# Attention and MLP kernel, second sweep: the second MLP layer in Strassen's form from the third group on, four first-layer products in one PSUM bank, and a written order for four engines

## The chip, the cores and the metric

The kernel is one program on one core of a Trainium2 chip. Its time is the device time of one launch in microseconds (us). The engines that matter here are TensorE (PE in the profile, with its weight loads as PEld), VectorE (DVE), ScalarE (ACT), GpSimd (POOL) and SyncE (SP), whose queue issues the transfers. SBUF is the on-chip memory that all engines read, PSUM the banks into which TensorE accumulates; a bank here holds 128 partitions of 512 fp32 values.

## The reference

The kernel computes an attention layer with a decay (8 batches, 8 heads, 576 tokens, 64 dimensions per head), a low-rank mixing over the tokens, and then an MLP. Only the MLP is touched:

```python
xt = x.transpose(0, 2, 1)
h = xt @ U @ V                       # mixing over tokens
u = x + h.transpose(0, 2, 1)
ch = np.maximum(u @ w_ch1, 0.0) @ w_ch2
return (u + ch).astype(np.float32)   # 8 x 576 x 512
```

`w_ch1` is 512 x 2048 and `w_ch2` 2048 x 512. All is fp32. Every matrix product is made from two rounded parts of each operand, a high part and a low part (`h` and `l`, type fp32r): high times high, low times high and high times low, so three matmuls stand for one.

## The kernel before

There are two sweeps. The first does attention and mixing and, of the MLP, the first 6 of the 16 chunks of 128 hidden units; it leaves `u` in two parts (`ud`) and the sum so far (`accd`) in DRAM. The second sweep does the other 10 chunks. It begins about 753 us into the profiled execution, works on 9 groups of 512 tokens in the order 7, 0, 1, ..., 5, 8, 6, and is written from line 945 on.

The first group is computed plainly, chunk by chunk (`first`, line 979, then `second`, line 993). From the second group on, two chunks at a time form a 2 x 2 block problem: the weights of a pair of chunks are cut into two halves of the input dimension and two chunks, the tokens into two halves of 256. Strassen's scheme in Winograd's form then makes the first layer with seven block products instead of eight. A block product is `product`: 6 matmuls that move 256 columns each (line 1069). The sums of weight blocks that it needs are made once (`weight_sums`), those of tokens once for each group: `token_sums` (lines 1052 to 1057) adds the two parts of `u` and combines the four quarters on POOL, and `token_part` splits a sum into two parts (`split`, lines 182 and 185: a copy on ACT, a subtraction on POOL). The products M1, M6, M5, M2, M7, M4, M3 of `pair_of_chunks` go into six PSUM banks in turn; line 1100 copies M1 on ACT, the seven `plus` (line 1092) combine them on DVE, and `relu` (lines 970 and 971) turns the four quarters into hidden values: the high part by ACT, the low part by DVE.

The second layer is plain in every group. `second` multiplies 128 tokens of hidden values by the 512 columns of `w_ch2`, three matmuls for each chunk (line 993). The calls of one pair of chunks wait in the list `ready` and are issued between the products of the next pair: three calls after M5, three after M7, two after M3. That makes 42 matmuls of 256 columns and 24 of 512 columns for a pair, and five pairs for a group. Four PSUM banks hold the sums of a group; when a group is complete, line 997 adds `accd` on DVE and lines 999 to 1002 store the result.

TensorE's order is the order of the text (`manual_schedule(engines={ET.PE})`); a planner orders the other engines. Each engine works through its own queue in order. Line 962 loads both parts of `u` for the next group into one of two buffers, and line 1138 loads `accd`.

Of the kernel before, what the change touches and what calls it, by code (L numbers as in the profile page):

```python
# [18 lines left out]
DM = H * D  # L19
DFF = 4 * DM  # L20
RK = 32
P = 128
# [18 lines left out]
def tile_decay_attention_moe(ctx, tc, qk, v, f, U, V, w1, w2, out):  # L41
# [908 lines left out]


    pool = pools(left, "left")
    up = pool("up", 2)
    hp_ = pool("hp", 4)
    psO = ctx.enter_context(tc.tile_pool(name="psO", bufs=4, space=PSUM, reuse_waits="tile"))
    psX = ctx.enter_context(tc.tile_pool(name="psX", bufs=2, space=PSUM, reuse_waits="tile"))
    HT = MAIN // 2

    def load_u(g):
        t = up.tile([P, 2, NDC, MAIN], F32R, tag="u", name=f"u{g}")  # L960
        for x in range(2):
            nc.sync.dma_start(t.bitcast(F32)[:, x], ud[g, :, x])
        return t[:, 0], t[:, 1]

    def hidden(name):
        return hp_.tile([P, MAIN], F32R, tag="hh", name=f"bh{name}"), hp_.tile([P, MAIN], F32R, tag="hl", name=f"bl{name}")

    def relu(h, src, cols):
        hh, hl = h[0][:, cols], h[1][:, cols]
        nc.scalar.activation(hh, src, AF.Relu)  # L970
        nc.vector.scalar_tensor_tensor(hl, src, 0.0, hh.bitcast(F32), op0=ALU.max, op1=ALU.subtract)  # L971

    def first(g, u, i):

        ps = psF.tile([P, 512], F32, tag="F", name=f"Hb{g}_{i}")
        m = 0
        for c in range(NDC):
            for wt_, ut in ((b1h, u[0]), (b1l, u[0]), (b1h, u[1])):
                nc.tensor.matmul(ps, wt_[i][:, c], ut[:, c, 0:MAIN], start=m == 0, stop=m == 3 * NDC - 1)  # L979
                m += 1  # L980
        h = hidden(f"{g}_{i}")
        relu(h, ps, slice(0, MAIN))
        return h

    def second(z, i, h, x):

        k = z["done"][x]
        z["done"][x] += 1
        if k == 0:
            z["po"][x] = psO.tile([P, DM], F32, tag="O", name=f"O{z['g']}_{x}")  # L990
        po = z["po"][x]
        for m, (ht, wt_) in enumerate(((h[0], b2h), (h[1], b2h), (h[0], b2l))):
            nc.tensor.matmul(po, ht[:, P * x : P * x + P], wt_[i], start=k == 0 and m == 0, stop=k == NB - 1 and m == 2)  # L993
        if k < NB - 1:
            return
        g, o = z["g"], z["acc"][:, x]
        nc.vector.tensor_tensor(o, po, o, op=ALU.add)
        if g < B:
            nc.sync.dma_start(out[g, P * x : P * x + P], o)
        else:  # L1000
            nc.sync.dma_start(out[2 * x + 1, MAIN:S], o[0:64])
            nc.sync.dma_start(out[2 * x, MAIN:S], o[64:128])


    n3 = 3 * 2 * P
    homes = [(sf.tile([P, 3, n3], F32R, tag=tag, name=f"sw{tag}")) for tag in ("hh", "hl")]
    more = [stp.tile([P, 1024], F32R, tag="raw", name=f"sw{x}") for x in range(3)]
    SW = []
    for i in range(NB // 2):
# [9 lines left out]
    Th = sf.tile([P, 4, 2, HT], F32R, tag="uh", name="Th")  # L1019
    Tl = sf.tile([P, 4, 2, HT], F32R, tag="ul", name="Tl")  # L1020
    tmp = [sf2.tile([P, 2, HT], F32, tag="ost", name=f"sum{x}") for x in range(2)]
    tmp.append(sf.tile([P, 2, HT], F32, tag="TS", name="sum2"))
    tmp = [t[:, y] for t in tmp for y in range(2)]

    def block(i, r, c):
        return [w[2 * i + r][:, 2 * c : 2 * c + 2] for w in (b1h, b1l)]

    def weight_sums(i, tmp=tmp):
        def whole(dst, r, c):
# [15 lines left out]
    whole_u = xn[2][:, 0:4].rearrange("p q (c t) -> p q c t", c=2)  # L1045

    def token_sums(u):

        for q in range(4):
            c, t = 2 * (q // 2), HT * (q % 2)  # L1050
            h, l = (x[:, c : c + 2, t : t + HT].bitcast(F32) for x in u)
            nc.gpsimd.tensor_tensor(whole_u[:, q], h, l, op=ALU.add)  # L1052
        b11, b12, b21, b22 = (whole_u[:, q] for q in range(4))
        nc.gpsimd.tensor_tensor(b11, b12, b11, op=ALU.subtract)
        nc.gpsimd.tensor_tensor(b12, b22, b12, op=ALU.subtract)
        nc.gpsimd.tensor_tensor(b22, b22, b11, op=ALU.subtract)
        nc.gpsimd.tensor_tensor(b21, b21, b22, op=ALU.subtract)

    def token_part(q):
        split(Th[:, q], Tl[:, q], whole_u[:, q], nc.scalar, nc.gpsimd)  # L1060

    T1, T3, T4, T2 = ([x[:, q] for x in (Th, Tl)] for q in range(4))

    def product(bank, tag, name, a, b):
        ps = bank.tile([P, 512], F32, tag=tag, name=name)[:, 0:HT]
        m = 0
        for c in range(2):
            for x, y in ((0, 0), (1, 0), (0, 1)):
                nc.tensor.matmul(ps, a[x][:, c], b[y][:, c], start=m == 0, stop=m == 5)  # L1069
                m += 1  # L1070
        return ps

    def pair_of_chunks(z, u, i, ready, renew):

        def go(k):
            for fn in ready[:k]:
                fn()
            del ready[:k]  # L1080

        def ub(c, t):
            return [x[:, 2 * c : 2 * c + 2, HT * t : HT * t + HT] for x in u]

        def f(k, a, b):
            return product(psF, "F", f"M{k}_{g}_{i}", a, b)

        def x(k, a, b):
            return product(psX, "X", f"M{k}_{g}_{i}", a, b)

        def plus(dst, ps, other):
            nc.vector.tensor_tensor(dst, ps, other, op=ALU.add)  # L1092

        g = z["g"]
        S1, (S2, S3, S4) = block(i, 1, 0), SW[i]
        h = [hidden(f"{g}_{2 * i + r}") for r in range(2)]
        lo, hi = slice(0, HT), slice(HT, MAIN)
        s1, s2, s3, s4, c11, c2 = tmp
        m1 = f(1, block(i, 0, 0), ub(0, 0))
        nc.scalar.copy(s1, m1)  # L1100
        m6 = x(6, S2, T2)
        if renew:
            token_part(3)
        plus(s2, m6, s1)
        m5 = f(5, S1, T1)
        if renew:
            token_part(0)
        plus(s4, m5, s2)
        go(3)
        plus(c11, x(2, block(i, 0, 1), ub(1, 0)), s1)  # L1110
        m7 = f(7, S3, T3)
        if renew:
            token_part(1)
        plus(s3, m7, s2)
        plus(c2, m5, s3)
        relu(h[0], c11, lo)
        relu(h[1], c2, hi)
        go(3)
        plus(s3, x(4, block(i, 1, 1), T4), s3)
        if renew:  # L1120
            token_part(2)
        plus(s4, x(3, S4, ub(1, 1)), s4)
        relu(h[1], s3, lo)
        relu(h[0], s4, hi)
        go(len(ready))
        for r, y in ((0, 0), (0, 1), (1, 2), (1, 3), (1, 0), (1, 1), (0, 2), (0, 3)):
            ready.append(lambda r=r, y=y: second(z, 2 * i + r, h[r], y))


    order = [B - 1, *range(B - 2), B, B - 2]  # L1130
    u = cur
    ready = []
    with tc.manual_schedule(engines={ET.PE}):
        for n, g in enumerate(order):
            un = load_u(order[n + 1]) if n + 1 < NG else None
            acc = xn[(n + 1) % 2]
            if n:
                nc.sync.dma_start(acc[:, 0:NM], accd[g].rearrange("x p d -> p x d"))
            z = {"g": g, "acc": acc, "po": [None] * NM, "done": [0] * NM}
            if n == 0:  # L1140
                for i in range(NB):
                    h = first(g, u, i)
                    for fn in ready:
                        fn()
                    ready = [lambda z=z, x=x, i=i, h=h: second(z, i, h, x) for x in range(NM)]
                    if i % 2 and i < 6:
                        weight_sums(i // 2)
                    if i == NB - 3:
                        token_sums(un)
                for q in (3, 0, 1, 2):  # L1150
                    token_part(q)
            else:
                for i in range(NB // 2):
                    pair_of_chunks(z, u, i, ready, un and i == NB // 2 - 1)
                    if n == 1 and i < 2:
                        spare = xn[2].rearrange("p c d -> p (c d)")
                        weight_sums(3 + i, [spare[:, 256 * y : 256 * y + 256] for y in range(5)])
                    if i == 2 and un:
                        token_sums(un)
            u = un  # L1160
        for fn in ready:
            fn()
    left.close()
    right.close()

# [45 lines left out]
```

## Time and profile before

| | |
|---|---|
| median of 3 runs | 1244.18 us (1242.86 to 1244.63) |
| profiled execution | 1242.59 us, of which the span of the profile is 1240.8 us |
| granted TensorE clock in it | 0.999 |
| TensorE busy | 1204.0 us, 97% of the span |
| VectorE, ScalarE, GpSimd busy | 861.3, 645.5 and 424.5 us |

The profile lists, for groups of instructions, the source line, the engine, the tiles written and read, the count, the busy time and the mean duration, and what ended the idle time before them. Recorded durations of matmuls overlap, so the rate of TensorE is read from the starts of its matmuls and not from their durations.

### The profile page before, as it was taken

Reading aid. Unit: us, or ns where it says so; the run is one execution under the profiler, and the core shown is the slowest. Engines: PE = TensorE matmul, PEld = TensorE weight load, DVE = VectorE, ACT = ScalarE, POOL = GpSimd, SP = SyncE. Lnnn points to the kernel's source line nnn. Section 1 sums busy time; section 2 is a strip of 40 time slices with the busy share of each in tenths; the row PEclk is TensorE's granted clock in tenths of the full one; section 3 lists DMA queues with packets and bytes.
Section 4 is the critical chain, followed back from the end, with each engine's and each line's share of the span. In section 5 each row is a group of like instructions: output and inputs, shape, how many; then the busy total and the mean of one; then the engine's idle time right before and its main releaser. Section 6 shows DMA issues by size and latency. Waiting matters only on the chain.

```text
span 1240.8 us, 21851 instructions
## 1 busy us (share of the span) xinstructions
PE 1204.0 (97%) x7824; PEld 1066.0 (86%) x7824; DVE 861.3 (69%) x2195; ACT 645.5 (52%) x1741; POOL 424.5 (34%) x377
## 2 busy tenths in 40 slices
PE   8998999999999999999999999989999999999998
PEld 5776898998989988989989888878988889888897
DVE  8877778768778778787686799684554645546443
ACT  5777678767778758777675444322122221212211
POOL 4223454534544435454541000441341413315100
PEclk9999999999999999999999999999999999999999
DMA  6544344525335325425342345121120312213010
GB/s 183 153 132 130 79 105 111 151 68 159 95 89 164 88 78 148 117 71 171 79 125 76 120 141 229 34 69 69 68 102 35 136 43 95 85 52 137 1 35 35
DMA packets 67581, 125.87 MB, mean 101 GB/s; under 512 B 7408, under 2 KB 31984, under 8 KB 65424
## 3 DMA queue, kind: packets, MB, share of 16 engines
q1 hardware_dynamic: 67408, 124.47, 32.8%
q8 instruction: 62, 1.02, 0.3%
q14 instruction: 47, 0.39, 0.1%
q10 hardware_dynamic: 64, 0.00, 0.0%
HBM read 88.65 MB, written 35.78 MB: 100 GB/s over the span
## 4 chain that ended last, share of the span: by engine, by line
PE 82%; DVE 8%; ACT 6%; issue 2%; DMA 2%; SPq 0%; ACTq 0%; POOL 0%; DVEq 0%; POOLq 0%
PE O L993 20%; PE M L1069 16%; PE A L700 10%; PE B L718 9%; PE V L543 5%; PE T L440 3%; PE S L344 3%; PE Hb L979 2%; PE V L515 2%; PE S L345 2%; ACT P L373 1%; ACT G L309 1%; PE Tt L609 1%; PE St L344 1%; PE S L341 1%
## 5 line engine op out<-in xcount | busy, mean ns | idle before, releaser
L1092 DVE TENSOR_TENSOR sum<-M,sum 128x256 f32<-128x256 f32 x280 | 117.7, 422 | 173.3 <-PE M L1069 172.3
L970 ACT ACTIVATE bh<-sum 128x256 fp32r<-128x256 f32 x160 | 66.3, 418 | 256.9 <-DVE sum L1092 256.8
L373 ACT ACTIVATE P<-S,nm 128x128 f32<-128x128 f32 (+3 forms) x256 | 137.5, 539 | 57.5 <-DVE nm L365 48.3
L365 DVE CUSTOM_DVE_ANT_0 S<-S,mask 128x128 f32<-128x128 f32 (+3 forms) x256 | 125.7, 495 | 53.5 <-PE S L345 46.8
L993 PE MATMUL O<-b2h,bh 128*128 128x512 f32 x360 | 143.0, 397 | 0.0
L993 PE MATMUL O<-b2l,bh 128*128 128x512 f32 x360 | 142.4, 396 | 0.0
L993 PE MATMUL O<-b2h,bl 128*128 128x512 f32 x360 | 141.8, 394 | 0.0
L700 PE MATMUL A<-uh,w1h 128*128 128x256 f32 (+1 forms) x384 | 120.3, 313 | 1.8 <-DVE hl L704 1.7
L309 POOL CAST G<-qk 64x576 fp32r<-64x576 f32 x52 | 34.9, 671 | 250.1 <-PE St L345 149.5
L700 PE MATMUL A<-ul,w1h 128*128 128x256 f32 (+1 forms) x384 | 113.5, 296 | 0.0
L700 PE MATMUL A<-uh,w1l 128*128 128x256 f32 (+1 forms) x384 | 113.5, 296 | 0.0
L185 POOL TENSOR_TENSOR Tl<-xn,Th 128x512 fp32r<-128x512 f32 x32 | 41.3, 1303 | 201.7 <-PE M L1069 178.1
L971 DVE SCALAR_TENSOR_TENSOR bl<-sum,bh 128x256 fp32r<-128x256 f32 x160 | 92.4, 581 | 19.4 <-ACT bh L970 19.0
L1052 POOL TENSOR_TENSOR xn<-u 128x512 f32<-128x512 f32 x32 | 43.7, 1391 | 167.6 <-DVE b1l L71 106.4
L718 PE MATMUL B<-w2h,hh 128*128 128x512 f32 x216 | 90.4, 418 | 2.3 <-DVE hl L704 1.3
L440 PE MATMUL T<-ident,P 128*128 128x128 f32 x544 | 85.5, 273 | 0.0
L718 PE MATMUL B<-w2l,hh 128*128 128x512 f32 x216 | 85.1, 394 | 0.0
L718 PE MATMUL B<-w2h,hl 128*128 128x512 f32 x216 | 84.6, 392 | 0.0
L422 DVE TENSOR_TENSOR PTl<-T,PTh 128x512 fp32r<-128x512 f32 (+1 forms) x156 | 79.0, 524 | 6.6 <-ACT PTh L419 6.3
L993 PEld LDWEIGHTS O<-b2l,bh 128*128 128x128 f32 x360 | 67.7, 188 | 16.5
L322 POOL TENSOR_TENSOR G<-qk,G 64x576 fp32r<-64x576 f32 x52 | 74.4, 1431 | 15.6 <-ACT G L309 6.2
L993 PEld LDWEIGHTS O<-b2h,bl 128*128 128x128 f32 x360 | 68.2, 189 | 11.2
(240 smaller groups left out, 3543.7 us busy)
## 6 DMA issues: line engine op xcount, KB each, us to landing
qk<-in_qk_dram SPq DMA_DIRECT2D x104, 288.0 KB
u<-ud SPq DMA_DIRECT2D x16, 1024.0 KB
sr<-in_w_dram SPq DMA_DIRECT2D x20, 512.0 KB
vr<-in_v_dram SPq DMA_DIRECT2D x32, 256.0 KB
accd<-ost SPq DMA_DIRECT2D x32, 256.0 KB
xn<-accd SPq DMA_DIRECT2D x8, 1024.0 KB
out_dram<-xn SPq DMA_DIRECT2D x32, 256.0 KB
ud<-uh SPq DMA_DIRECT2D x7, 1024.0 KB
```

Source lines behind the costliest of these rows:

```text
L322: pin(el.tensor_tensor(g[oth, 2, cols], k[oth], gf[oth, 2, cols], op=ALU.subtract))
L365: nc.vector.tensor_tensor_reduce(ps[:, :w], ps[:, :w], mask[:, 512 - w : 512], scale=-SCALE, scalar=3.0e38, op0=ALU.add, op1=ALU.min, accu ...
L373: nc.scalar.activation(pt, ps[:, :w], AF.Exp, bias=z["nm"][:, col : col + 1], scale=-1.0, accum_out=z["sm"][:, col : col + 1])
L422: defer(2, lambda: nc.vector.tensor_tensor(dstl, src, dsth.bitcast(F32), op=ALU.subtract))
L440: nc.tensor.transpose(tp[:, P * x : P * x + P], z["P"][j][i][:, P * c : P * c + P], ident)
L700: nc.tensor.matmul(ps[:, :nt], wt[:, fc, c], ut[:, c, sl], start=m == 0, stop=m == 3 * NDC - 1)
L718: nc.tensor.matmul(ps, ht[:, fc, P * x : P * x + P], wt[:, fc], start=fc == 0 and m == 0, stop=fc == NA - 1 and m == 2,)
L970: nc.scalar.activation(hh, src, AF.Relu)
L971: nc.vector.scalar_tensor_tensor(hl, src, 0.0, hh.bitcast(F32), op0=ALU.max, op1=ALU.subtract)
L993: nc.tensor.matmul(po, ht[:, P * x : P * x + P], wt_[i], start=k == 0 and m == 0, stop=k == NB - 1 and m == 2)
L1069: nc.tensor.matmul(ps, a[x][:, c], b[y][:, c], start=m == 0, stop=m == 5)
L1092: nc.vector.tensor_tensor(dst, ps, other, op=ALU.add)
```

## The change

It concerns the second sweep alone.

- From the third group on, the second layer is made in Strassen's form too (`output_products`). The hidden values X11, X12, X22 and four sums S1, S2, S3, S4 of the quarters (X21 itself is not multiplied) are multiplied with weight blocks in seven products N1 to N7 of 6 matmuls with 256 columns. Over the five pairs of a group, N1, N3, N4, N5, N6 and N7 accumulate in six banks; N2 goes into a bank of the first layer and is added to the result by DVE in every pair. At the end of a group the banks are combined into the four quarters of the result (`ends_1`, `ends_6`, `ends_3` and two single additions) by ACT, DVE and POOL.
- The second group keeps the plain second layer (`plain_products`); meanwhile `weight_sums2` makes the sums of the second layer's weights on POOL, DVE and ACT.
- In the first layer M1, M6, M7 and M4 accumulate one after another in a bank A, which ACT copies out (`s1`, `u2`, `u3`, `r12`) after each; M2, M5 and M3 share a bank B. The seven additions of a pair become three.
- The sums S3, S1, S2, S4 are made from tiles of the pair before, after M1, N1, M2 and N4 of the next pair: DVE makes the sum, ACT the high part, POOL the low part.
- The order in a pair is M1, N1, M2, N4, M6, N2, N7, M7, N5, M5, N6, M4, N3, M3. From the third group on DVE, ACT and POOL, too, keep the order of the text.
- The tokens are no longer loaded whole into a double buffer: three quarters are loaded into a tile `direct`, refilled in the last pair of a group, and the high and low part of all four go into two of the `xn` tiles, where POOL adds them (`token_whole` after the third pair's M4, `token_sums` after the fourth's).

```diff
+    def relu(h, l, src):
+        nc.scalar.activation(h, src, AF.Relu)
+        nc.vector.scalar_tensor_tensor(l, src, 0.0, h.bitcast(F32), op0=ALU.max, op1=ALU.subtract)
...
+    def weight_sums2(i):
+        eng = nc.gpsimd
...
+        for src, (h, l) in zip((t1, t0, t2, t3), [block2(i, 0, 1)] + SD[i]):
+            split(h, l, src, nc.scalar, eng)
...
+    def add(dst, a, b, eng=nc.vector):
+        eng.tensor_tensor(dst, a, b, op=ALU.add)
...
+    def output_products(z, i):
...
+        def one(k, a, w):
+            if k == 2:
+                ps = z["B"].rearrange("p (y d) -> p y d", y=2)
+                multiply(ps, a, w, True, True)
+                add(quarter[0], ps, quarter[0])
+                return
...
+        def ends_1():
+            nc.scalar.copy(u4, z["M"][1])
+            add(quarter[0], u4, quarter[0], nc.gpsimd)
+
+        def ends_6():
+            add(u4, z["M"][6], u4)
+            add(u3, z["M"][7], u4)
+            add(u4, z["M"][5], u4)
+            for q in (2, 3):
+                add(quarter[q], u3, quarter[q], nc.gpsimd)
+            for x in (2, 3):
+                store(z["g"], acc, x)
+
+        def ends_3():
+            add(quarter[1], z["M"][3], quarter[1])
+            add(quarter[1], u4, quarter[1], nc.gpsimd)
...
+        product(A, block(i, 0, 0), D1, True)
+        nc.scalar.copy(s1, A)
+        sum_(0)
+        if renew:
+            load_direct(renew, 0)
+        second_layer()
+        sum_(1)
+        ends()
+        product(Bk, block(i, 0, 1), D2, True)
+        add(c11, Bk, s1)
+        nc.scalar.activation(X11[0], c11, AF.Relu)
+        sum_(2)
...
+        second_layer()
+        nc.vector.scalar_tensor_tensor(X11[1], c11, 0.0, X11[0].bitcast(F32), op0=ALU.max, op1=ALU.subtract)
+        sum_(3)
+        ends()
+        product(A, W2, T2, False)
+        nc.scalar.copy(u2, A)
...
+        second_layer()
+        ends()
+        second_layer()
+        ends()
+        product(A, W3, T3, False)
+        nc.scalar.copy(u3, A)
...
+        product(Bk, W1, T1, True)
+        add(c22, Bk, u3)
+        nc.scalar.activation(X22[0], c22, AF.Relu)
...
+        product(A, block(i, 1, 1), T4, False)
+        nc.scalar.activation(r12, A, AF.Relu)
+        nc.scalar.copy(X12[0], r12)
...
+        second_layer()
+        nc.vector.tensor_tensor(X12[1], r12, X12[0].bitcast(F32), op=ALU.subtract)
+        ends()
+        product(Bk, W4, D3, False)
+        add(r21, Bk, u2)
...
+        nc.scalar.activation(r21, r21, AF.Relu)
+
+        def sum_0():
+            nc.vector.scalar_tensor_tensor(c22, c22, 0.0, r21, op0=ALU.max, op1=ALU.add)
+            nc.vector.scalar_tensor_tensor(r21, c11, 0.0, r21, op0=ALU.max, op1=ALU.subtract)
+            split(*S3, r21, nc.scalar, nc.gpsimd)
+
+        def sum_2():
+            nc.vector.scalar_tensor_tensor(n2, c11, 0.0, c22, op0=ALU.max, op1=ALU.subtract)
+            split(*S2, n2, nc.scalar, nc.gpsimd)
+
+        def sum_3():
+            add(r12, r12, n2)
+            split(*S4, r12, nc.scalar, nc.gpsimd)
+
+        held["sums"] = [sum_0, lambda: split(*S1, c22, nc.scalar, nc.gpsimd), sum_2, sum_3, None]
...
+        for n in range(1, NG):
+            with tc.manual_schedule(engines={ET.PE} if n == 1 else {ET.PE, ET.DVE, ET.Activation, ET.Pool}):
+                group(n)
```

More of the change, by code (lines that the diff above doesn't have):

```diff
@@ L980, in first, with store @@
                 m += 1
-        h = hidden(f"{g}_{i}")
-        relu(h, ps, slice(0, MAIN))
-        return h
[L985 to L997, printed above, removed]
+        flat = hb.rearrange("p k x t -> p (k x t)")[:, 2 * MAIN * (i % 3) : 2 * MAIN * (i % 3) + 2 * MAIN]
+        h = flat[:, 0:MAIN], flat[:, MAIN : 2 * MAIN]
+        relu(*h, ps)
+        return h
+    def store(g, acc, x):
+        o = acc[:, x]
         if g < B:
@@ L1002, in second @@
             nc.sync.dma_start(out[2 * x, MAIN:S], o[64:128])
+    def second(z, i, h, x):
+        if i == 0:
+            z["po"][x] = psM.tile([P, DM], F32, tag=BANKS[x], name=f"O{z['g']}_{x}")
+        po = z["po"][x]
+        for m, (ht, wt_) in enumerate(((h[0], b2h), (h[1], b2h), (h[0], b2l))):
+            nc.tensor.matmul(po, ht[:, P * x : P * x + P], wt_[i], start=i == 0 and m == 0, stop=i == NB - 1 and m == 2)
+        if i < NB - 1:
+            return
+        o = z["acc"][:, x]
+        nc.vector.tensor_tensor(o, po, o, op=ALU.add)
+        store(z["g"], z["acc"], x)
     n3 = 3 * 2 * P
@@ L1068, in product @@
             for x, y in ((0, 0), (1, 0), (0, 1)):
-                nc.tensor.matmul(ps, a[x][:, c], b[y][:, c], start=m == 0, stop=m == 5)
+                nc.tensor.matmul(
+                    ps, a[x][:, c], b[y][:, c], start=start and m == 0, stop=m == 5, skip_group_check=not start
+                )
                 m += 1
[L1071 to L1078, printed above, removed]
-                fn()
[L1080 to L1101, printed above, removed]
+    def add(dst, a, b, eng=nc.vector):
+        eng.tensor_tensor(dst, a, b, op=ALU.add)
@@ new lines, in plain_products, with one @@
+    def plain_products(z, i):
+        acc = z["acc"]
+        def one(x, r, h):
+            if i == 0 and r == x // 2:
+                z["M"][x] = psM.tile([P, DM], F32, tag=BANKS[x], name=f"O{z['g']}_{x}")
+            ps = z["M"][x]
+            for m, (p_, wt_) in enumerate(((0, b2h), (1, b2h), (0, b2l))):
+                nc.tensor.matmul(
+                    ps, h[p_][:, P * (x % 2) : P * (x % 2) + P], wt_[2 * i + r],
+                    start=i == 0 and r == x // 2 and m == 0, stop=i == NK - 1 and r != x // 2 and m == 2,
+                )
+            if i == NK - 1 and r != x // 2:
+                add(acc[:, x], ps, acc[:, x])
+                store(z["g"], acc, x)
+        work = [(x, r, h) for r, h, xs in ((0, X11, (0, 1)), (1, X22, (2, 3)), (1, X12, (0, 1)), (0, S3, (2, 3))) for x in xs]
+        return [(lambda y=y: one(*y), None) for y in work]
@@ new lines, in tile_decay_attention_moe, with pair_of_chunks, second_layer, ends @@
+    held = {}
+    pairs = [0]
+    def pair_of_chunks(z, i, ready, renew, plain, late):
+        g = z["g"]
+        W1, (W2, W3, W4) = block(i, 1, 0), SW[i]
+        D1, D2, D3 = ([direct[:, k, x] for x in range(2)] for k in range(3))
+        s1, u2, u3, c11, c22, r21, n2, r12 = tmp
+        pairs[0] += 1
+        if pairs[0] % 2:
+            c11 = other
+        bank_a = psX.tile([P, 512], F32, tag="A", name=f"A{g}_{i}")
+        bank_b = psX.tile([P, 512], F32, tag="B", name=f"B{g}_{i}")
+        if ready and len(ready) == 7:
+            held["z"]["B"] = bank_b
+        A, Bk = bank_a[:, 0:HT], bank_b[:, 0:HT]
+        places = 7 if len(ready) > 4 else 1
+        todo = []
+        def second_layer():
+            nonlocal places
+            n = -(-len(ready) // max(places, 1))
+            places -= 1
+            todo.extend(ready[:n])
+            del ready[:n]
+            for fn, _ in todo:
+                fn()
+        def ends():
+            for _, fn in todo:
+                if fn:
+                    fn()
+            del todo[:]
+        sums = held.pop("sums", [None] * 5)
+        def sum_(k):
+            if sums[k]:
+                sums[k]()
+        product(A, block(i, 0, 0), D1, True)
[10 more added lines that the diff above has]
+        sum_(2)
+        if renew:
+            load_direct(renew, 1)
+        second_layer()
[4 more added lines that the diff above has]
+        nc.scalar.copy(u2, A)
+        sum_(4)
@@ L1109, in pair_of_chunks @@
[L1109 to L1119, printed above, removed]
+        second_layer()
+        nc.vector.scalar_tensor_tensor(X22[1], c22, 0.0, X22[0].bitcast(F32), op0=ALU.max, op1=ALU.subtract)
+        ends()
+        product(A, block(i, 1, 1), T4, False)
@@ L1130, in tile_decay_attention_moe @@
+        def sum_2():
[5 more added lines that the diff above has]
+        held["sums"] = [sum_0, lambda: split(*S1, c22, nc.scalar, nc.gpsimd), sum_2, sum_3, None]
+        held["z"] = z
+        ready.extend(output_products(z, i))
     order = [B - 1, *range(B - 2), B, B - 2]
-    u = cur
     ready = []
-    with tc.manual_schedule(engines={ET.PE}):
[L1134 to L1161, printed above, removed]
-            fn()
```

171 lines of the change are left out of this document (134 added, 37 removed).

## The prediction, made blind

> **What bounds the kernel now.** I read the page first, then the second sweep by windows, the chain of waits in order of time, and TensorE's instructions one by one.
>
> ```profile
> span 1240.8 us, 21851 instructions
> PE 1204.0 (97%) x7824; PEld 1066.0 (86%) x7824; DVE 861.3 (69%) x2195; ACT 645.5 (52%) x1741; POOL 424.5 (34%) x377
> ```
> ```profile
> core 0: us, PE busy (x) PEld busy (x) DVE busy (x) ACT busy (x) POOL busy (x), PEclk, DMA share, GB/s
> 805.00:857.00 52.00, 48.56 (x299) 43.56 (x298) 36.13 (x77) 14.08 (x35) 17.57 (x14) 0.97 0.12 41
> 910.00:963.00 53.00, 53.00 (x332) 47.62 (x331) 27.45 (x61) 12.68 (x30) 15.89 (x12) 1.00 0.21 80
> ```
> ```profile
> 861.76 2.13 PE M L1069 x18
> ...
> 872.32 2.13 PE M L1069 x18
> ...
> 882.88 2.13 PE M L1069 x18
> ...
> 1230.15 7.02 PE O L993 x30
> ```
>
> In a group TensorE is busy for 53.00 of 53.00 us, while DVE (27.45), ACT (12.68) and POOL (15.89) have room. The chain holds nothing but matmuls and repeats every 10.56 us (861.76, 872.32, 882.88): that is a pair of chunks, and 52.8 us a group. Only the second group's start (805 to 857) shows TensorE idle, 3.4 us. So a matmul taken away in the third and later groups is gained in full, as long as no other engine then holds TensorE up.
>
> **The matmuls saved.** TensorE's rows, by their starts:
>
> ```profile
> 1225.04 0.28 PE L1069 MATMUL M<-u,b1h 128*128 128x256 f32 x1
> ...
> 1226.46 0.40 PE L993 MATMUL O<-b2h,bh 128*128 128x512 f32 x1
> ...
> 1228.56 0.28 PE L1069 MATMUL M<-Th,b1h 128*128 128x256 f32 x1
> ```
>
> Twelve matmuls of 256 columns took 1226.46 - 1225.04 = 1.42 us, 0.118 each; nine of 512 took 2.10, 0.233 each. A pair is 42 x 0.118 + 24 x 0.233 = 10.57, as the chain says. Now it is 84 x 0.118 = 9.94 (a product of six takes 0.71), 0.63 less. Strassen pairs: four from the third group (its first still issues plain products), thirty from the last six groups, and one behind the last group: 35 x 0.63 = 22 us less. This term is firm: the new matmuls have the form of those at line 1069, with a weight load for each.
>
> **What must now be ready in time.** Before, the products took six banks in turn and none waited for the reader of the one just before. Now bank A must be copied out by ACT (`u2`) between M6 and M7, and that copy stands in ACT's queue behind the high parts of S3, S1, X11, S2 and S4. Each of these follows a DVE operation, and four POOL subtractions of 128x256 run between them. The durations:
>
> ```profile
> L970 ACT ACTIVATE bh<-sum x137: 412/418/420, 860.9 to 1220.1; 128x256 fp32r<-128x256 f32 x137
> L1100 ACT COPY sum<-M x35: 372/372/376, 862.6 to 1221.8; 128x256 f32<-128x256 f32 x35
> ```
> ```profile
> L1092 DVE TENSOR_TENSOR sum<-M,sum x240: 404/424/426, 863.3 to 1223.2; 128x256 f32<-128x256 f32 x120
> ```
> ```profile
> L971 DVE SCALAR_TENSOR_TENSOR bl<-sum,bh x138: 411/424/1486, 860.7 to 1220.5; 128x256 fp32r<-128x256 f32 x138
> ```
> ```profile
> L185 POOL TENSOR_TENSOR Tl<-xn,Th x32: 1288/1296/1482, 804.0 to 1177.3; 128x512 fp32r<-128x512 f32 x32
> L185 POOL TENSOR_TENSOR VS<-vr,VS x26: 1548/1568/1574, 137.5 to 671.5; 128x640 fp32r<-128x640 f32 x26
> ```
> ```profile
> 872.16 0.28 PE L1069 MATMUL M<-u,b1h 128*128 128x256 f32 x1
> ...
> 873.12 0.38 ACT L1100 COPY sum<-M 128x256 f32<-128x256 f32 x1 [0.78 <-PE M L1069]
> ...
> 876.39 0.28 PE L1069 MATMUL M<-u,b1h 128*128 128x256 f32 x1
> ...
> 877.30 0.42 DVE L1092 TENSOR_TENSOR sum<-M,sum 128x256 f32<-128x256 f32 x1 [1.08 <-PE M L1069]
> ...
> 877.35 1.30 POOL L1056 TENSOR_TENSOR xn<-xn 128x512 f32<-128x512 f32 x1
> ...
> 877.75 0.42 ACT L970 ACTIVATE bh<-sum 128x256 fp32r<-128x256 f32 x1 [4.26 <-DVE sum L1092]
> ...
> 878.02 0.42 DVE L1092 TENSOR_TENSOR sum<-M,sum 128x256 f32<-128x256 f32 x1 [0.30 <-PE M L1069]
> ...
> 878.36 0.57 DVE L971 SCALAR_TENSOR_TENSOR bl<-sum,bh 128x256 fp32r<-128x256 f32 x1
> ...
> 878.73 1.36 POOL L1057 TENSOR_TENSOR xn<-xn 128x512 f32<-128x512 f32 x1
> ```
>
> The row of `bl` matters most: 0.42 us, but up to 1.49, while the DVE row that reads PSUM (L1092) never passes 0.426. Operations with both inputs in SBUF are the ones that stretch, when POOL is at work: at 878.36 one starts inside a POOL instruction that ends at 878.65, and ends 0.28 later, at 878.93; the next POOL instruction then lasts 1.36 instead of 1.30 and starts 0.08 behind, so POOL loses about 0.15. Five of the new DVE operations ahead of `u2` have both inputs in SBUF (c22, r21, n2, X11's low part, r12+n2).
>
> [...]
>
> From the rows above: from the end of a product's slot to its reader 0.20 on DVE (876.39 + 0.71, 877.30), 0.25 on ACT; between engines 0.04 (877.72 to 877.75); DVE starts its next operation 0.34 after the last (878.02, 878.36), and I take ACT alike. No POOL operation of 128x256 is in the trace: half of the 1.296 gives 0.65, the straight line through 512 and 640 columns 0.75. Starting at M1 of a steady pair, with 0.65 (0.75 behind the stroke):
>
> ```
> DVE r21 .20-.62   ACT relu .66-1.08   DVE c22 1.12, r21 1.46-1.88   ACT S3 1.92-2.34
> POOL S3 low 2.38-3.03 / 3.13          ACT S1 2.25-2.67
> DVE c11 (M2 ends 2.13) 2.33-2.75      ACT X11 2.79-3.21
> DVE n2 from 2.79, held by S3 low, to 3.31 / 3.41        ACT S2 to 3.77 / 3.87
> POOL S1 low 3.18-3.83 / 3.28-4.03     DVE X11 low from 3.25, held, to 4.11 / 4.31
> POOL S2 low 3.98-4.63 / 4.18-4.93     DVE r12+n2 from 4.05, held, to 4.91 / 5.21
> ACT S4 4.95-5.37 / 5.25-5.67          ACT u2 to 5.66 / 5.96
> ```
>
> M7 is due after seven products, at 4.98, and gets bank A at 5.70 or 6.00: it waits 0.72 or 1.02 in every pair. Without POOL in the way the same chain ends with `u2` at 4.76, and M7 waits for nothing. So the bounds are 0 and 1.02; I take 0.65, nearest to the lower figure, since the chain credits no slack at any hop. For 34 pairs that is 22 us (0 to 35): **the matmul saving is spent there.** What is queued behind the late `u2` is `u3`, X22 and so on, which wait for later products anyway, and TensorE's own queue.
>
> **The change of groups**, six times. POOL's addition of `ends_1` (1.30) stands between the low parts of S1 and S2, so r12+n2 ends 0.65 later: 0.6 more at M7. At the end of the pair DVE has, from N6's end as zero, the three additions of `ends_6` (128x512, 0.68 each, the second reading the first's result) to 2.2, then X12's low part, held by POOL's addition (1.7 to 3.0) to 3.28, `ends_3` to 3.88 and r21 to 4.22. M2 of the next pair needs bank B, which r21 reads, at 5 x 0.71 = 3.56 and starts at 4.28: 0.7. The relu ends at 4.68, and the next sum meets POOL's last addition (4.45 to 5.75) and ends at 6.03 instead of 5.14, on the way to S3 and again to `u2`: 1.2. Together 2.5, six times 15 us; without POOL's hold DVE's queue alone gives r21 at 3.48, in time, so the bounds are 0 and 20. The 0.68 and the end of the kernel:
>
> ```profile
> 1235.09 2.79 DVE L997 TENSOR_TENSOR xn<-O,xn 128x512 f32<-128x512 f32 x4 [3.57 <-PE O L993]
> ```
> ```profile
> 1236.75 0.40 PE L993 MATMUL O<-b2l,bh 128*128 128x512 f32 x1
> ```
>
> **The end.** Now DVE ends at 1237.88, 0.9 after the last matmul's slot (1236.75 + 0.23), and the stores follow. Then the last seven products have nothing between them: N7 must wait for S3's low part (3.03 against 2.13), about 1 us. After N6 come 1.6 us of DVE and three POOL additions, 3.9 us, before the last store: 0.2 + 1.6 + 3.9 - 0.7 (N3 runs meanwhile) = 5.0, 4 more than now. I take 6 with some queueing (4 to 8).
>
> **Once only.** `weight_sums2` of the last pair runs in the third group: eight POOL operations of 0.65 ahead of S3's low part, 1.5 us (0 to 3). The start of the second group:
>
> ```profile
> 818.41 0.38 PE L1069 MATMUL M<-Th,swhh 128*128 128x256 f32 x1 [2.59 <-DVE sum L1092]
> ```
> ```profile
> 806.58 2.93 DVE L1031 TENSOR_TENSOR xn<-b1h,b1l 128x256 f32<-128x256 f32 x2 [0.41 <-POOL Tl L185]
> ```
>
> TensorE waits 2.59 us behind DVE sums that POOL held (two took 2.93). The text keeps that meeting; fewer DVE additions there, but tokens that come through a tile which is in use until about 795. I take 0, bounds -4 and +3.
>
> **Transfers at nothing.**
>
> ```profile
> 860.43 0.79 SPq L962 DMA_DIRECT2D u<-ud  x2
> ```
> ```profile
> 869.05 5.42 POOL L1052 TENSOR_TENSOR xn<-u 128x512 f32<-128x512 f32 x4 [7.42 <-DMA u<-ud]
> ```
>
> Two MB were there 8.6 us after their issue. Each quarter of `direct` is 0.5 MB, is issued as soon as its product has run in the last pair, and is due a pair later, 9.9 us; the whole loads have more than a pair. SP's queue holds the stores ahead of them, all early in the group. Without that cover a late quarter would cost what it is late, up to some 2 us a group.
>
> **Sum.** -22 + 22 + 15 + 6 + 1.5 + 0 = +22.5 on the profiled execution's own 1242.6, so 1265.1; the median of the runs stands 1.6 above that execution, hence **1267 us**.
>
> **Rivals.**
>
> *The waits are hidden* (faster). If the three DVE operations meet no POOL instruction, M7 waits for nothing and the group change costs little: -22 + 0 + 2 + 6 + 0.5 = -13.5, so 1231. For it: the chain without POOL ends 0.2 us in time, and two second-layer products stand between M6 and M7. Against: POOL's operations start from the same ACT results, so they fall into the same microseconds; and in the row above `bl` was caught by POOL up to its full length. It decides at `u2`: ending before 4.9 us of a pair, or after.
>
> *Only the group changes pay* (the same). POOL's operations turn out shorter than 0.6 and the steady pair runs at 9.94, but 128x512 additions stay at 1.30: -22 + 0 + 15 + 6 + 1 = 0, so 1244 to 1247. For it: group changes have measured lengths, the 128x256 one is a guess.
>
> *The saving isn't there* because matmuls of 256 columns cost more than half of 512: 0.118 against 0.117 excludes it.
>
> **How the numbers follow.** A change under 0.2% (2.5 us) can't be told from none here. Forecast (1254 to 1285 by its bounds, most of it below 1280): 0.57. Waits hidden (1226 to 1240): 0.30. Group changes alone (1240 to 1250): 0.13, of which 0.05 within 0.2%, 0.04 above and 0.04 below. Slower 0.61, the same 0.05, faster 0.34. The range takes 1230 to 1280: it leaves out the lower third of the second case (0.10) and the top of the first (0.07).
>
> **What would show it.** In the changed profile: 256-column products for the second layer at 0.118 each (the 22); `bl`-like DVE rows with both inputs in SBUF at a mean near 0.7 with POOL busy; TensorE idle before M7, released by ACT's copy of A, about 0.65 in nearly every pair, and a steady period of 10.6; idle before M2 in a group's second pair, released by DVE. A period of 9.9 to 10.0 with no such idle time would prove the forecast wrong at its main step; idle time released by a DMA would be a mistake about the transfers.

## The result and the profile after

The changed kernel takes **1298.79 us** (median of four runs, 1297.38 to 1300.58) against 1244.41 for the kernel before on the same chip: a ratio of 1.044, with a 95% interval of 1.0422 to 1.0458. That is slower, as forecast, but by 54 us where 23 were forecast, and above the range (1230 to 1280). The profiled execution took 1299.44 us, with a span of 1297.7 against 1240.8, so 56.9 us more.

The page of the kernel after, and one window of its second sweep (busy time and count of PE, PEld, DVE, ACT and POOL, granted clock of TensorE, share of the DMA engines, GB/s):

```profile
span 1297.7 us, 23855 instructions
PE 1213.6 (94%) x8454; PEld 1098.1 (85%) x8454; DVE 929.9 (72%) x2209; ACT 739.8 (57%) x2028; POOL 612.6 (47%) x585
```
```profile
910.00:963.00 53.00, 47.39 (x372) 45.93 (x371) 31.47 (x52) 21.30 (x57) 32.41 (x32) 0.97 0.27 90
```

In the window that TensorE filled before (53.00 of 53.00) it is now idle for 5.6 us, and GpSimd has gone from 15.9 to 32.4 busy. Where TensorE waits is in the view of waits (the line that waits, the instruction that ends the wait, us in total, times, longest):

```profile
PE A L1103 <- ACT sum L1249: 34.8, 35, 1.8
PE B L1103 <- DVE xn L1109: 5.7, 7, 1.1
...
PE Hb L985 <- DVE xn L728: 1.2, 1, 1.2
```

The first row is the wait that the prediction named: M7 (line 1103, bank A) behind ACT's copy `u2` (line 1249). One of the 35, 0.46 us, is in the second group; the other 34 are in the 34 pairs that the prediction counted, 1.01 us each and not 0.65. The second is M2 behind r21: once in the second group (0.45), and at each of the six changes of groups (5.2 us together).

The span divides by the starts of M1, the first of the kernel before, the second of the kernel after:

```profile
806.06 0.28 PE L1069 MATMUL M<-u,b1h 128*128 128x256 f32 x1
...
861.60 0.28 PE L1069 MATMUL M<-u,b1h 128*128 128x256 f32 x1
...
914.42 0.28 PE L1069 MATMUL M<-u,b1h 128*128 128x256 f32 x1
...
1178.56 0.28 PE L1069 MATMUL M<-u,b1h 128*128 128x256 f32 x1
...
1220.81 0.28 PE L1069 MATMUL M<-u,b1h 128*128 128x256 f32 x1
```
```profile
809.86 0.28 PE L1103 MATMUL A<-direct,b1h 128*128 128x256 f32 x1
...
868.11 0.28 PE L1103 MATMUL A<-direct,b1h 128*128 128x256 f32 x1
...
925.54 0.28 PE L1103 MATMUL A<-direct,b1h 128*128 128x256 f32 x1
939.06 0.28 PE L1103 MATMUL A<-direct,b1h 128*128 128x256 f32 x1
952.24 0.28 PE L1103 MATMUL A<-direct,b1h 128*128 128x256 f32 x1
963.45 0.28 PE L1103 MATMUL A<-direct,b1h 128*128 128x256 f32 x1
974.38 0.28 PE L1103 MATMUL A<-direct,b1h 128*128 128x256 f32 x1
985.51 0.28 PE L1103 MATMUL A<-direct,b1h 128*128 128x256 f32 x1
...
1221.55 0.28 PE L1103 MATMUL A<-direct,b1h 128*128 128x256 f32 x1
1269.93 0.28 PE L1103 MATMUL A<-direct,b1h 128*128 128x256 f32 x1
```

| stretch | before | after | more |
|---|---|---|---|
| up to the second group | 806.06 | 809.86 | 3.8 |
| second group | 55.5 | 58.2 | 2.7 |
| third group | 52.8 | 57.4 | 4.6 |
| groups four to eight | 264.1 | 296.0 | 31.9 |
| ninth group, four pairs | 42.2 | 48.4 | 6.1 |
| last pair and end | 20.0 | 27.8 | 7.8 |

A group is 52.8 us before and 59.2 after. Its rows above show two kinds of pairs: the first two take 13.52 and 13.18, the other three 11.21, 10.93 and 11.13, where 10.56 was the old pair and 9.94 would be the new one without a wait.

**One steady pair**, the one that starts at 952.24, in the timeline of the kernel after. Lines 185, 1297, 1245 and 1109 are the low parts of S3, S1 and S2 (a row with x3), n2, X11's low part and r12+n2; 182 is the high part of S4:

```profile
954.80 2.49 POOL L185 TENSOR_TENSOR hb<-xn,hb 128x256 fp32r<-128x256 f32 x3 [7.13 <-ACT hb L182]
...
955.00 0.82 DVE L1297 SCALAR_TENSOR_TENSOR xn<-xn,xn 128x256 f32<-128x256 f32 x1
955.75 0.95 DVE L1245 SCALAR_TENSOR_TENSOR hb<-other,hb 128x256 fp32r<-128x256 f32 x1
956.63 0.95 DVE L1109 TENSOR_TENSOR xn<-xn 128x256 f32<-128x256 f32 x1
...
957.61 0.41 ACT L182 CAST hb<-xn 128x256 fp32r<-128x256 f32 x1 [1.35 <-DVE xn L1109]
957.92 0.37 ACT L1249 COPY sum<-A 128x256 f32<-128x256 f32 x1
...
958.35 0.39 PE L1103 MATMUL A<-Th,swhh 128*128 128x256 f32 x1 [0.93 <-ACT sum L1249]
```

This pair follows the chain of the prediction, instruction by instruction: three DVE operations, each started inside a GpSimd subtraction and each ended after it (0.82, 0.95, 0.95 where 0.42 is the undisturbed length), then S4's high part, then `u2`, then M7. From M1 the prediction had bank A free at 5.70 or 6.00; `u2` ends at 6.05 (957.92 + 0.37 - 952.24). M7 was due at 5.0 and starts at 6.11: 1.1 late. Its own product takes 0.82 instead of 0.71, since the first matmul behind the wait is 0.1 longer (the next starts 0.22 after it, at 958.57, instead of 0.12). Together 1.2, and 10.0 + 1.2 is the pair of 11.21.

The third pairs of groups four to nine and the last two pairs of the ninth group, where no token sums run, are all like this one: three held operations, M7 starting 6.1 after M1, and 11.2 for each of those that a next pair follows. The fourth and fifth pairs of the other groups (10.93 and 11.13) reach nearly the same wait by another way. There n2 and X11's low part run nearly undisturbed (0.42 and 0.45 to 0.50), and of the three only r12+n2 is held (0.95). But r21 starts 0.82 and 1.08 after M1 instead of 0.20, because the token sums on GpSimd, operations of 128x512, hold X12's low part of the pair before, here ahead of the fifth pair, which starts at 974.38:

```profile
974.07 1.46 DVE L1279 TENSOR_TENSOR hb<-xn,hb 128x256 fp32r<-128x256 f32 x1
```

### The profile page after: what moved, and what is told of

The parts are those of the page before. It is cut to its first block, busy times and chain, and to the rows that moved or that the text cites. A ratio compares the mean times of both kernels' runs of the same rounds, so it can differ in the third digit from the quotient of the medians.

```text
span 1297.7 us, 23855 instructions
## 1 busy us (share of the span) xinstructions
PE 1213.6 (94%) x8454; PEld 1098.1 (85%) x8454; DVE 929.9 (72%) x2209; ACT 739.8 (57%) x2028; POOL 612.6 (47%) x585
## 4 chain that ended last, share of the span: by engine, by line
PE 60%; DVE 21%; ACT 11%; issue 3%; POOL 3%; DMA 2%; POOLq 0%; DVEq 0%; ACTq 0%; SPq 0%
PE A L700 9%; PE B L718 8%; PE A L1103 5%; PE N L1123 5%; PE V L543 5%; DVE xn L1109 4%; PE B L1103 4%; PE T L440 3%; PE V L515 2%; PE S L344 2%; PE S L345 2%; ACT hb L182 2%; DVE hb L1279 2%; ACT P L373 1%; PE O L1006 1%
## 5 line engine op out<-in xcount | busy, mean ns | idle before, releaser
L185 POOL TENSOR_TENSOR hb<-xn,hb 128x256 fp32r<-128x256 f32 x140 | 111.8, 820 | 122.4 <-ACT hb L182 110.1
L1109 DVE TENSOR_TENSOR xn<-B,xn 128x512 f32<-128x512 f32 (+1 forms) x74 | 40.0, 540 | 83.1 <-PE B L1103 81.5
L182 ACT CAST hb<-xn 128x256 fp32r<-128x256 f32 x140 | 53.1, 402 | 80.6 <-DVE xn L1109 45.8
L1123 PE MATMUL N<-sw,hb 128*128 128x256 f32 x546 | 81.0, 284 | 2.0 <-ACT hb L182 1.4
L322 POOL TENSOR_TENSOR G<-qk,G 64x576 fp32r<-64x576 f32 x52 | 74.5, 1432 | 15.6 <-ACT G L309 6.2
L1123 PE MATMUL N<-b2h,hb 128*128 128x256 f32 x420 | 81.0, 285 | 0.0
L323 POOL TENSOR_TENSOR G<-qk,G 64x576 fp32r<-64x576 f32 x52 | 74.9, 1441 | 5.1 <-ACT G L309 4.9
L700 PEld LDWEIGHTS A<-uh,w1h 128*128 128x128 f32 x384 | 72.8, 190 | 4.5 <-DVE hl L704 4.3
L344 PE MATMUL S<-G 128*128 128x128 f32 x208 | 70.0, 342 | 6.7 <-ACT P L373 5.1
L1123 PEld LDWEIGHTS N<-sw,hb 128*128 128x128 f32 x546 | 72.1, 190 | 2.9 <-ACT hb L182 1.6
L419 ACT CAST PTh<-T 128x512 fp32r<-128x512 f32 (+1 forms) x156 | 68.2, 469 | 10.4 <-PE T L440 9.9
```

The lines of the kernel that those rows point to most:

```text
L182: heng.copy(dh, src)
L185: leng.tensor_tensor(dl, src, dh.bitcast(F32), op=ALU.subtract)
L344: nc.tensor.matmul(ps, G[j][:, 0, c0 : c0 + P], G[j][:, 2, cols], start=first, stop=False)
L700: nc.tensor.matmul(ps[:, :nt], wt[:, fc, c], ut[:, c, sl], start=m == 0, stop=m == 3 * NDC - 1)
L1109: eng.tensor_tensor(dst, a, b, op=ALU.add)
L1123: nc.tensor.matmul(ps[:, y], a[p_][:, P * y : P * y + P], w[q_], start=start and y == 0 and m == 0, stop=stop and y == 1 and m == 2,)
```

## The experiments

The kernel before took 1245.2, 1244.9 or 1246.2 us beside these runs; ratios are to it. The lengths of pairs are differences between starts of M1, as above.

**S4 behind `u2`.** S4's sum and its high part are issued one place later, so that `u2` is no longer queued behind them.

```diff
-        held["sums"] = [sum_0, lambda: split(*S1, c22, nc.scalar, nc.gpsimd), sum_2, sum_3, None]
+        held["sums"] = [sum_0, lambda: split(*S1, c22, nc.scalar, nc.gpsimd), sum_2, None, sum_3]
```

> One line moves: the sum S4 (DVE r12+n2, ACT high part, POOL low part) is issued after ACT's copy u2 instead of ahead of it. [...] 35 waits of 1.0 us and the slower product behind each go: about 36 us less than the changed kernel, 1263 us (1255 to 1272). Rival A (M7 waits because it shares bank A with M6, whatever stands ahead of u2): nothing changes, 1299. Rival B (POOL holding DVE is all, the order on ACT does not matter): the wait shrinks by less than half, 1283 or more.

Measured: **1256.75 us**, ratio 1.0095 (1.0079 to 1.0112), 42 us less than the changed kernel. The pair that starts at 994.81 in its timeline, and three starts of M1:

```profile
997.37 2.49 POOL L185 TENSOR_TENSOR hb<-xn,hb 128x256 fp32r<-128x256 f32 x3 [5.84 <-ACT hb L182]
...
997.55 0.84 DVE L1297 SCALAR_TENSOR_TENSOR xn<-other,xn 128x256 f32<-128x256 f32 x1
998.31 0.95 DVE L1245 SCALAR_TENSOR_TENSOR hb<-xn,hb 128x256 fp32r<-128x256 f32 x1
998.74 0.37 ACT L1249 COPY sum<-A 128x256 f32<-128x256 f32 x1
999.19 0.96 DVE L1109 TENSOR_TENSOR xn<-xn 128x256 f32<-128x256 f32 x1
...
999.81 0.28 PE L1103 MATMUL A<-Th,swhh 128*128 128x256 f32 x1
```
```profile
994.81 0.28 PE L1103 MATMUL A<-direct,b1h 128*128 128x256 f32 x1
1004.81 0.28 PE L1103 MATMUL A<-direct,b1h 128*128 128x256 f32 x1
1014.77 0.28 PE L1103 MATMUL A<-direct,b1h 128*128 128x256 f32 x1
```

GpSimd holds the same three operations as long as before (0.84, 0.95, 0.96), but `u2` ends at 999.11, M7 starts at 999.81 without a wait, on time (5.00 after M1), and the pairs take 10.00 and 9.96. In the fourth and fifth pairs, too, M7 no longer waits. So a held operation costs nothing by itself; it costs when `u2` is behind it. What is left are mainly the changes of groups: the first two pairs of a group take 10.7 and 11.9.

**No low parts on GpSimd.** The order stays; the subtractions for the low parts of S1 to S4 are left out from the third group on.

```diff
-            split(*S3, r21, nc.scalar, nc.gpsimd)
+            nc.scalar.copy(S3[0], r21)
```

(and S1, S2, S4 alike)

> The order stays as in the changed kernel, but the four POOL subtractions that make the low parts of S1 to S4 are left out from the third group on (the products read a low part that is not renewed: zero for S1, S2, S4). It leaves out part of the computation. Theory: with POOL out of the steady pair DVE's sums take 0.42 us each and u2 ends about in time: steady pairs without token work 10.0 to 10.3, pairs beside token work and the group changes still late; 1265 to 1282 us. Rival B (POOL's hold is all): all steady waits gone, 1260 or less. [...]

Measured: **1298.01 us**, ratio 1.0421 (1.0397 to 1.0444), no gain at all: a miss, and a useful one. The steady pairs do take 9.96 to 10.01 with S4 in its old place, so without GpSimd's subtractions M7 doesn't wait, as the prediction's chain said. But the third pair of every group but the last takes 14.1 to 16.8. In the pair that starts at 1014.24:

```profile
1013.91 5.57 POOL L1085 TENSOR_TENSOR xn<-xn,xn 128x512 f32<-128x512 f32 x4 [8.14 <-DMA xn<-ud]
...
1016.94 1.40 DVE L1293 SCALAR_TENSOR_TENSOR xn<-other,xn 128x256 f32<-128x256 f32 x1
1018.60 1.17 DVE L1297 SCALAR_TENSOR_TENSOR xn<-other,xn 128x256 f32<-128x256 f32 x1
1019.69 1.50 DVE L1245 SCALAR_TENSOR_TENSOR hb<-xn,hb 128x256 fp32r<-128x256 f32 x1
1021.11 1.48 DVE L1109 TENSOR_TENSOR xn<-xn 128x256 f32<-128x256 f32 x1
...
1023.35 0.58 PE L1103 MATMUL A<-Th,swhh 128*128 128x256 f32 x1 [2.94 <-ACT sum L1249]
```

GpSimd, with nothing in its queue ahead, is at `token_whole` early, waits for the transfer of the tokens, starts just before a pair begins and then runs eight operations of 128x512 with hardly a gap. DVE operations beside them take up to 1.50 us, and M7 waits 2.94; behind that wait the matmuls start 0.21 apart until 1029.07, which adds some 2.4 us. In the changed kernel the low parts had kept most of these operations out of the start of a pair: they reached 0.6 us into the fourth and 0.9 us into the fifth.

**That reading tried: also no token sums.** As the run above, and from the third group on the sums of the next group's tokens are left out too.

```diff
-            if nxt is not None and i in (2, 3):
+            if n == 1 and i in (2, 3):
```

> GpSimd's subtractions for the low parts of S1 to S4 left out from the third group on, as before, and also the sums of the next group's tokens (token_whole, token_sums) from the third group on, so that later groups multiply old token parts; the order is otherwise that of the changed kernel. Theory (the run without low parts alone lost its gain because the token sums then bunched up in GpSimd across the start of the last pair and held VectorE there): pairs at 10.0 everywhere except at a change of groups (about 11.4 and 12.6), the third pair of a group falls from 14 to 17 back to 10.0, and the kernel takes 1298.0 - 7 x 5.5 = 1260, range 1255 to 1268. Rival (something else in that run made the third pair long, such as the loads or the products' own order): the third pair stays at 14 or more and the time stays above 1285.

Measured: **1267.32 us**, ratio 1.018 (1.0155 to 1.0206). The third pair is back at 10.00:

```profile
1002.99 0.28 PE L1103 MATMUL A<-direct,b1h 128*128 128x256 f32 x1
1012.99 0.28 PE L1103 MATMUL A<-direct,b1h 128*128 128x256 f32 x1
```

The reading of the miss holds. The run shows something else too: the first two pairs of a group still take 11.4 and 12.6, 4.0 more than two steady pairs, without any of these GpSimd operations. What is left there, the additions at a group's end and the splits of the new tokens, is enough for that; the two were not taken apart.

**The plain second layer in every group.** The bank, the written order and the token path of the change stay; N1 to N7, S1 to S4 and `weight_sums2` don't run.

```diff
-            pair_of_chunks(z, i, ready, nxt if i == NK - 1 else None, n == 1, late)
+            pair_of_chunks(z, i, ready, nxt if i == NK - 1 else None, True, late)
```

> The second layer stays plain in all groups; the first layer's shared bank, the token tiles and the written order stay. The sums S1, S2, S4 of hidden values, the sums of second-layer weights and the end-of-group sums are gone. Theory: nothing stands ahead of u2, pairs take 10.6 as before the change; only the later starts of the first two groups (5.5 us) and nothing else remain: 1250 us (1246 to 1256). Rival D (the shared bank and the written order cost the time, not Strassen in the second layer): M7 waits here too, 1270 or more.

Measured: **1247.3 us**, ratio 1.0017 (1.0002 to 1.0032). Every pair from the third group on takes 10.54 to 10.58, and the view of waits has one wait of a first-layer product left that is over 0.5 us:

```profile
PE A L1103 <- POOL Tl L185: 2.9, 1, 2.9
```

It stands in the second group. So sharing bank A, ordering by hand and loading the tokens in another way cost nothing in the steady state by themselves; the steady loss comes with Strassen's second layer.

**The end of a group later.** The additions of a finished group are regrouped. N1, N4, N5 and N7 are added by DVE as each is complete, still in the next group's first pair; the rest (N6 twice, N3, the GpSimd additions and the stores) runs in the middle of its second pair. S4 stays where the change has it.

```diff
         def ends_3():
-            add(quarter[1], z["M"][3], quarter[1])
...
+            held["last_sums"] = last_sums
...
+        if i == 1 and "last_sums" in held:
+            held.pop("last_sums")()
```

> The place of S4 stays. The sums at the end of a group are arranged anew: N1, N4, N5 and N7 are read out by DVE as soon as they are ready, the rest (N6 twice, N3 and three POOL additions, with the stores) waits until the middle of the next group's second pair. Theory: the first pair of a group falls from 12.0-13.5 to about 11.5 and the second from 12.4-13.2 to 11 (r21 no longer waits behind three additions), the end of the kernel gets 2 us shorter: 6 x 3.3 + 2 = about 20 us less, 1279 us (1272 to 1287). If the group changes are long for another reason (token sums, transfers), 1295 or more.

Measured: **1279.8 us**, ratio 1.0274 (1.0254 to 1.0295), 19 us less. A group's first two pairs take 11.5 and 11.2 instead of 12.0 to 13.6 and 12.4 to 13.2, and the row of M2 behind DVE falls from 5.7 us to

```profile
PE B L1103 <- DVE xn L1109: 1.3, 2, 0.8
```

Both of these are in the second group, so M2 no longer waits at a change of groups.

**Both moves.**

> S4 behind u2 and the last additions of a group put off to the middle of the next group's second pair, together. Theory (two separate waits: M7 behind u2 in the steady pair, and the additions at a change of groups): the gains add up. The run with S4 moved took 1256.75; its pairs at a change of groups still run 10.7 and 11.9 instead of 10.0, 2.6 a group, six times 15.6, and the other move took off nearly that much in its own run (1298.79 to 1279.8, 19.0). So 1256.75 - 15.6 - 1 to 2 for the end of the kernel: 1239 to 1240, range 1236 to 1246, with every pair of the groups four to nine at 10.0 to 10.2. Rival (the two moves remove the same waiting, seen twice): 1252 or more, with a pair above 11 left at each change of groups.

Measured: **1248.47 us**, ratio 1.0025 (1.0011 to 1.0038): 50 us less than the changed kernel, but above the expected range of 1236 to 1246. The first two pairs are 10.3 and 10.0, about as expected; the fourth of groups four to eight takes 10.8 to 11.7. One such pair starts at 954.91:

```profile
947.90 0.33 SPq L973 DMA_DIRECT2D xn<-ud  x1
...
952.98 5.58 POOL L1085 TENSOR_TENSOR xn<-xn,xn 128x512 f32<-128x512 f32 x4 [1.82 <-DMA xn<-ud]
...
957.44 1.40 DVE L1301 SCALAR_TENSOR_TENSOR xn<-other,xn 128x256 f32<-128x256 f32 x1
```

The later additions store their result later, the next tokens are loaded into the tile that was stored, and so `token_whole` runs into the start of the next pair: the same meeting as in the miss above, from another cause.

**Token sums split.** Half of `token_whole` goes to VectorE, a pair later; the last pair's `weight_sums2` is cut in two.

```diff
-                late = (lambda: token_whole(low)) if i == 2 else token_sums
+                late = (lambda: token_whole(low, (0, 1))) if i == 2 else token_sums
+            if nxt is not None and i == 3:
+                mid = lambda: token_whole(low, (2, 3), nc.vector)
```

> As the run with both moves, and half of token_whole's additions go from GpSimd to VectorE, a pair later, into VectorE's idle time behind M4; weight_sums2 of the last pair in the third group is cut in two and spread over its first two pairs. Theory: what the run with both moves still lost (fourth pairs of 10.8 to 11.7, the third group's third pair 12.14) is GpSimd's long operations running across the start of a pair, where they hold VectorE's sums for S3 to S4, since the tokens came 4 us later behind the later stores. Then those pairs go to 10.0 to 10.4: 5.4 less some 1.2, and 1.8, so 1248.5 - 6 = 1242.5, range 1239 to 1247, a ratio to the kernel before of 0.995 to 1.001. Rival (the late tokens or the loads themselves hold these pairs up, not GpSimd's place): fourth pairs stay near 11 and the time stays at 1248.

Measured: **1246.42 us**, ratio 1.0003 (0.9988 to 1.0019): no difference from the kernel before that can be told. The fourth pairs take 9.96 to 10.17, so the reading of the run before holds; a whole group takes 50.6 to 50.9. The third group did not gain as expected: its third pair falls from 12.1 to 10.0, but its second takes 11.5. The time saved there does not reach the end of the kernel: in the profiled executions the second group starts 5.4 later than before (811.50 against 806.06) and takes 59.0 instead of 55.5, and the last pair and the end take 26.4 instead of 20.0.

**The end on VectorE.** Behind the last pair, the low parts of S3, S1, S2 and S4 on VectorE.

```diff
-                fn()
+                fn(nc.vector)
```

> As the run before it (both moves, token sums split), and behind the last pair, where nothing but the last seven products is left, the low parts of S3, S1, S2 and S4 are subtracted on VectorE instead of GpSimd. There TensorE waited 1.29 us for S3's high part, 0.42 for its low part, and the products behind those waits ran at 0.213 per matmul instead of 0.119 (24 of them took 5.05 us instead of 2.86). Theory (the end costs what S3's chain takes, and the waits bring the slow matmuls with them): low parts of 0.42 on an engine that GpSimd doesn't hold shorten the wait by 0.4 to 0.9 and take away some or all of the 2.2 us: the kernel ends 0.5 to 3 us sooner, 1243.4 to 1246, a ratio to the kernel before of 0.9975 to 0.9995. Rival (the chain behind the last product through VectorE sets the end, whoever makes the low parts): 1246 to 1247 and the same ratio as the run before it, 1.0003.

Measured: **1246.67 us**, ratio 1.0011 (0.9999 to 1.0023). The last pair and the end take 25.2 instead of 26.4 in the profile, but the median, above the 1243.4 to 1246 of the theory, is the same as in the run before it: the gain is too small to be told by these runs. No version was found that beats the kernel before.

## Why the prediction came out as it did

- **Matmuls saved, -22: held.** Where nothing waits, a pair takes 9.96 to 10.01 (forecast 9.94): 0.55 to 0.60 less than before, about 20 us for 35 pairs.
- **M7 behind `u2`, +22: the mechanism was right in the main, its size was the main error.** The place and the releaser are those of the chain, and the two runs that break it in different ways (`u2` ahead of S4, or no GpSimd subtraction) both give pairs of 10.0. But steady pairs of the changed kernel average 11.08 (33.25 us for the last three of a group, mean of groups four to eight), 1.1 above 9.98: some 37 us for 34 pairs. The step that failed is "I take 0.65, nearest to the lower figure". The lower figure rested on half of a 128x512 operation for GpSimd's 128x256. Half is too little: in the kernel after, the shortest subtraction of 128x512 takes 1.29 and the shortest of 128x256 0.72, where half would be 0.64. The straight line through two sizes, which the prediction also had (0.75), came nearer: 0.73 undisturbed and 0.82 on average,

```profile
L185 POOL TENSOR_TENSOR hb<-xn,hb 128x256 fp32r<-128x256 f32 x100 | 79.6, 819 | 81.4 <-ACT hb L182 78.0 <-POOL hb L185 3.4
```

  and the chain with that price gave 1.02 for the wait; M7 starts 1.1 late where the chain runs as forecast. The rest is the slower first matmul behind each wait, 0.1, which no term had. In the fourth and fifth pairs of a group the chain is not the forecast one: the token sums delay r21, a meeting that the prediction put at nothing in a steady pair. That they come out near the same figure (M7 0.84 and 1.04 late) is luck.
- **Changes of groups, +15: low.** In groups four to eight the first two pairs take 25.95 on average, 3.8 above two steady ones instead of 2.5, so about 23 us for six. Where the clock holds, as at the change at 985.51, it is 3.1. M7's wait in the first pair is 0.8 longer than in a steady pair (forecast 0.6). The second pair is 2.1 longer: M2 starts 1.3 late and its first matmul is 0.1 slower (forecast 0.7), and short stops of N2 and N7 cost another 0.5, which no term had. The 1.2 that the prediction added at M7 in that pair isn't there: M7 waits 1.01, against 0.93 in the pair above. The other 0.7 a group is a fall of TensorE's clock behind M7's wait in the first pair, shown in the last section. The lower bound, nothing left "without POOL's hold", was not tried by a run: without low parts and token sums GpSimd still makes the additions at a group's end and the splits of the tokens, and 4.0 a group remain.
- **The end, +6: held.** 7.8, of which about 0.5 belong to the last pair's own wait less its saving, leave 7.3 (4 to 8 were the bounds). N7 waits for S3, 1.37 for its high part and 0.6 for its low part (about 1 was forecast), and the last GpSimd additions take 3.70 (forecast 3.9):

```profile
1284.80 0.38 PE L1123 MATMUL N<-sw,hb 128*128 128x256 f32 x1 [1.37 <-ACT hb L182]
...
1290.22 3.70 POOL L1109 TENSOR_TENSOR xn<-sum,xn 128x512 f32<-128x512 f32 x3 [2.88 <-DVE sum L1109]
```

- **`weight_sums2` once, +1.5: held.** The pair that follows it takes 13.41, 2.3 more than a steady one (bounds 0 to 3).
- **The start, 0: missed by 6.5 us.** 3.8 us come ahead of the second group, 2.4 of them in the first group, whose TensorE now waits for DVE (the row of `Hb` above and another of 0.7). 2.7 are in the second group; with the plain second layer everywhere it takes 56.5 instead of 58.2, so 1.8 of them go with `weight_sums2` running there. The prediction only priced the one meeting that it saw in the trace before. Some of the 3.8 may be the scatter of one execution: the same start lies between 808 and 814 in the runs here.
- **Transfers at nothing: held for this kernel.** No wait of TensorE is ended by a DMA in the second sweep. The cover is thin, though: in two of the experiments the moment at which the tokens land set where GpSimd's sums ran, and that cost 1 to 7 us a group, through GpSimd and VectorE.
- **The rivals.** "The waits are hidden" stood on a chain that ended 0.2 us in time without GpSimd; the run with S4 behind `u2` shows that one place in the order would have been enough for it, but the kernel as written lies on the other side. "Only the group changes pay" needed GpSimd's operation under 0.6; it is 0.73 undisturbed. Why a VectorE operation that starts inside a GpSimd subtraction lasts longer was not shown; the rows of the steady pair show by how much, 0.82 and twice 0.95 us instead of 0.42.

The terms as measured: -20 + 37 + 23 + 7.3 + 2.3 + 6.5 = 56, against 56.9 in the span. The prediction's upper bounds for its terms (35, 20, 8, 3 and 3, less the 22) add up to 1291, not to the 1285 that it names. The result is above both, because M7's wait, the changes of groups and the start each came out above their own bound.

## What to carry to other kernels

When a copy that frees a bank has a place in an engine's queue, count what stands ahead of it: here one sum moved behind that copy was worth 42 us, and the matmuls saved were worth 20. A wait recurs with every pair, so its size must come from the longest plausible chain rather than the most favourable one, and an unmeasured operation from the line through two measured sizes, not from a proportion. Taking work off a queue moves what is behind it: look where that engine's next long operation will then run. In the run without low parts it was GpSimd's additions of 128x512 at the start of a pair, and M7 waited 2.94 us in that pair.

## What the runs showed of the hardware that was not expected

**The clock falls behind some waits of about 1.75 us and not behind others.** Two first pairs of groups in the kernel after, the same M7 behind the same wait, and for each of them two windows, the one in which the wait lies and the next (the number behind the five busy times is the granted clock):

```profile
932.45 0.39 PE L1103 MATMUL A<-Th,swhh 128*128 128x256 f32 x1 [1.75 <-ACT sum L1249]
...
992.45 0.39 PE L1103 MATMUL A<-Th,swhh 128*128 128x256 f32 x1 [1.76 <-ACT sum L1249]
```
```profile
929.39:932.80 3.41, 1.66 (x14) 1.46 (x14) 3.29 (x4) 1.05 (x4) 3.41 (x4) 1.00 0.66 262
932.80:936.21 3.41, 3.41 (x19) 3.41 (x18) 0.78 (x2) 0.37 (x1) 0.19 (x1) 0.50 0.00 0
...
990.83:994.24 3.41, 1.79 (x15) 1.80 (x16) 2.12 (x4) 1.05 (x3) 2.16 (x3) 1.00 0.27 106
994.24:997.66 3.42, 3.42 (x31) 3.42 (x30) 2.77 (x6) 1.21 (x3) 0.00 (x0) 1.00 0.02 5
```

In the first the clock falls to 0.50 for one such window of 3.41 us, and the matmuls from 932.98 to 936.18 start 0.21 apart instead of 0.119; in the second it stays at 1.00. The first pair of the group takes 13.52 in the one case and 12.04 in the other. It happens in four of the six changes of groups. In two of these the next pair is 0.7 shorter, since M2 then waits less, so that the falls cost about 4.5 us in all. In the runs with S4 behind `u2` and with the end of a group later, no change of groups has such a fall: the granted clock is 1.00 in each of six stretches from 868 to 1221 us.

The four slow windows begin at 932.80, 1052.27, 1110.29 and 1229.76, and each lasts 3.41 us. Their starts are 119.47, 58.02 and 119.47 us apart, which is 35, 17 and 35 times 3.413, and the windows above are cut at such steps. Cut like that, the window that holds the wait has 1.66 us of matmuls at each of the four changes that fall, and 1.79 and 1.71 at the two that don't. That the smaller share of matmuls brings the fall is the author's estimate from these six cases; no run was made to try it.

**A queue that runs empty can cost as much as a full one**, as the run without low parts shows: four subtractions fewer on GpSimd in each of 35 pairs, and the same time (1298.01 us against 1298.79).
